# Top-32 attention and a tanh-shrink layer: GpSimd computes a step's threshold ahead of the preceding step's row sums, VectorE its reciprocal ahead of the selection rounds

## The chip, the cores and the metric

The kernel runs on one core of one Trainium2 chip. A core has TensorE (PE, matrix products into PSUM), VectorE (DVE), ScalarE (ACT), GpSimd (POOL) and SyncE (SP, which issues most DMAs). Each engine works through its own list of instructions in order, and semaphores make one engine wait for another. The metric is the time of one execution in device microseconds (us), as the median of several runs.

## The reference, cut to what matters

Batch 8, 8 heads, 576 rows, head width 64; the layer behind it has 4608 rows of 512, an inner width of 2048, and everything is float32.

```
scores = scale * np.matmul(q, k.transpose(0, 1, 3, 2))            # 576 x 576 per head
kth = np.partition(scores, -top_k, axis=-1)[..., -top_k:-top_k + 1]   # top_k = 32
scores = np.where(scores >= kth, scores, -1000000000.0)
scores = scores - np.max(scores, axis=-1, keepdims=True)
attn = np.exp(scores); attn = attn / (np.sum(attn, axis=-1, keepdims=True) + 1e-09)
attn_out = np.matmul(attn, v)
x = attn_out.transpose(0, 2, 1, 3).reshape(B * S, H * D)
h = x @ w_in
out = (h - np.tanh(h)) @ w_out
```

So every row of scores needs its 32nd largest value, and all that is below it is dropped before the softmax.

## The kernel before, in words

The work is cut into 144 steps. A step takes 128 rows of queries for a pair of heads, so its scores are a tile of 128 partitions by 2 x 576. The loop over n at L991 writes the instructions out by hand, in an order in which several steps are under way at once; what is recorded there is the order in which every engine works. In one turn n:

- `mask(n - 1)` (L386): GpSimd forms the threshold tb (L396, one instruction for each head of the pair) and the negative row maximum nb (L405) from the maxima m. ScalarE turns score and tb into a penalty with a Relu (L409), GpSimd subtracts it from the scores (L412), and then compares the selection's bounds with tb (bad, L416).
- `search(n)` (L340): VectorE forms pairwise maxima and minima of the scores (L359 to L367), takes the eight largest of six pieces (L371), and then runs four rounds of MAX8 (L378) and MATCH_REPLACE8 (L381), which give the 32 largest in m. After round i it calls `between(i)`. After round 0 that is `invert(n - 2)`, VectorE's reciprocal of the row sums (L451), and `divide(n - 2)`, ScalarE's multiplication by it (L458); after the last round it is `turn_z(n - 2)`, VectorE's block transpose of the result (L490).
- pieces of the feed-forward part, dealt by `deal` in portions of 0.4, 0.2, 0.2 and 0.2 of what is due in a step. They are matmuls (L606, and L719 for the second product, which is done in seven products of quarters), ScalarE's tanh and copy (L618, L619), GpSimd's subtraction (L620), its sums of quarters (L693) and its joins (L740).
- `scores(n + 1)` (L317): TensorE writes the scores of the next step into a single PSUM tile (L329), which VectorE frees at L367; ScalarE copies it to SBUF (L337).
- `expo(n - 1)` (L428): ScalarE's exponentials with row sums (L432), and GpSimd's addition of 1e-9 to the sums, which goes into rd (L442).
- every second step `values` (TensorE, L555) with weights that went out to DRAM and back through SP's queue in another order.

The steps of the first batch (`pe` is true, up to about 240 us) go another way after the exponentials: TensorE transposes them (L527), the reciprocal is L448, it is spread by GpSimd (L471), and GpSimd multiplies the result (L573). In that stretch the weights are also converted (L182 to L205).

The order on an engine matters here in this way: before the change GpSimd meets, between the subtraction of one step and the threshold of the next, first the bad comparison, then feed-forward work of the first portion, then rd of the step before, then feed-forward work of the later portions, and then tb:

```
            if here(-1):
                mask(n - 1, exact)          # tb, nb, Relu, subtraction of step n - 1
            if here(0):
                search(n, exact, between)   # m of step n
            ...
            if here(1):
                scores(n + 1)
            ...
            if here(-1):
                expo(n - 1)                 # exponentials and rd of step n - 1
```

## Time and profile before

| what | us |
|---|---|
| median of 3 runs | 1554.77 (1550.6 to 1556.14) |
| the profiled execution | 1556.96 |
| its span, first to last instruction | 1555.2 |
| mask on ScalarE, L409, x288 | 0.774 each (median) |
| threshold on GpSimd, L396, x288 | 0.300 each (median) |
| nb on GpSimd, L405, x144 | 0.248 each (median) |
| subtraction on GpSimd, L412, x288 | 1.413 each (median) |
| rd on GpSimd, L442, x144 | 0.227 each (median) |
| reciprocal on VectorE, L451, x126 | 0.151 each (median) |
| division on ScalarE, L458, x252 | 0.760 each (median) |
| transpose on VectorE, L490, x126 | 1.359 each (median) |

The times of single instructions come from the profiled execution, which is a little longer than the median. Busy times are shares of the span, and in a row of waits the first number is the sum of idle time in us before the instructions of a line, the second how often, the third the longest. In rows of the timeline the first number is the start, the second the duration of all that is merged in the row, and the bracket the idle time before it with what ended it. A step takes about 9.2 us in the middle of the kernel.

### The profile page before, as it was taken

How to read it: one execution, taken by the hardware profiler on the slowest of the kernel's cores; microseconds unless marked ns; L12 is line 12 of the kernel's file. 1: busy time of each engine (PE TensorE's matmuls, PEld its weight loads, DVE VectorE, ACT ScalarE, POOL GpSimd, SP SyncE). 2: the span in 40 equal slices, each digit the busy share in tenths (PEclk: the TensorE clock that was granted, in tenths of full speed). 3: DMA queues.
4: the chain of work that ended last, by engine and by line, in shares of the span. 5: the costliest groups of instructions: out<-in, count | busy, mean ns of one | idle time of the engine just before them, and what ended most of it. 6: DMA issues, size and time to landing. Idle time of an engine off the chain costs nothing.

```text
span 1555.2 us, 26814 instructions
## 1 busy us (share of the span) xinstructions
PE 1404.2 (90%) x7892; PEld 1068.5 (69%) x7892; DVE 1296.3 (83%) x4914; ACT 1015.9 (65%) x1898; POOL 1103.7 (71%) x1573
## 2 busy tenths in 40 slices
PE   4677997899998999989989999999998989999998
PEld 2455655666766767766767777777776767778887
DVE  7998898899999999898988899989999888883000
ACT  4766775776776767776766777777776766674311
POOL 3777689868677686858686868686877686767523
PEclk9778999999999999999999999999999999999999
DMA  9945113677667576575766666667575666643311
GB/s 264 365 172 176 26 34 106 157 192 161 187 158 189 145 167 166 155 198 139 191 156 164 158 173 159 172 153 197 150 180 149 156 153 160 169 142 95 96 44 43
DMA packets 257178, 241.70 MB, mean 155 GB/s; under 512 B 193536, under 2 KB 201728, under 8 KB 249856
## 3 DMA queue, kind: packets, MB, share of 16 engines
q1 hardware_dynamic: 255248, 239.69, 58.0%
q8 instruction: 65, 1.06, 0.3%
q14 instruction: 89, 0.73, 0.2%
q10 hardware_dynamic: 1776, 0.22, 0.1%
HBM read 153.99 MB, written 85.85 MB: 154 GB/s over the span
## 4 chain that ended last, share of the span: by engine, by line
PE 30%; DVE 26%; POOL 16%; ACT 16%; issue 5%; DMA 5%; SPq 0%; DVEq 0%; ACTq 0%; POOLq 0%
PE hps L606 11%; PE hx L719 6%; PE hy L719 6%; DVE m L378 4%; POOL g L620 4%; ACT z L458 4%; DVE top L371 4%; ACT z L409 4%; POOL z L412 4%; POOL g L693 3%; PE av L555 3%; PE scps L329 3%; DVE zx L490 3%; ACT z L432 3%; DVE rest L381 3%
## 5 line engine op out<-in xcount | busy, mean ns | idle before, releaser
L606 PE MATMUL hps<-xT,w_in 128*128 128x256 f32 (+1 forms) x2176 | 479.1, 377 | 11.5 <-ACT g L619 10.3
L606 PEld LDWEIGHTS hps<-xT,w_in 128*128 128x128 f32 x2176 | 396.9, 195 | 92.0 <-issue 23.5
L412 POOL TENSOR_TENSOR z<-sc,z 128x576 f32<-128x576 f32 x288 | 404.6, 1427 | 74.2 <-ACT z L409 74.2
L409 ACT ACTIVATE z<-sc,tb 128x576 f32<-128x576 f32 x288 | 207.6, 768 | 246.7 <-POOL tb L396 232.6
L620 POOL TENSOR_TENSOR g<-g,th 128x512 f32<-128x512 f32 x144 | 183.2, 1273 | 100.4 <-ACT g L619 99.4
L490 DVE STREAM_TRANSPOSE zx<-z 128x1152 f32<-128x1152 f32 x126 | 172.0, 1365 | 88.6 <-ACT z L458 86.5
L432 ACT ACTIVATE z<-z,nb 128x576 f32<-128x576 f32 x288 | 221.8, 776 | 2.3 <-POOL z L412 2.3
L458 ACT ACTIVATE z<-z,rd 128x576 f32<-128x576 f32 x252 | 180.4, 763 | 55.2 <-DVE rd L451 53.7
L329 PE MATMUL scps<-kT,qT 64*128 64x288 f32 (+1 forms) x1120 | 161.6, 439 | 42.4 <-DVE top L367 35.6
L371 DVE MAX8 top<-ab 128x8 f32<-128x144 f32 x864 | 193.9, 292 | 0.0
L337 ACT COPY sc<-scps 128x1152 f32<-128x1152 f32 x144 | 160.7, 1116 | 21.2 <-PE scps L329 20.8
L378 DVE MAX8 m<-rest 128x8 f32<-128x168 f32 x576 | 160.2, 318 | 0.0
L329 PEld LDWEIGHTS scps<-kT,qT 64*128 64x128 f32 (+1 forms) x1120 | 88.5, 180 | 96.9 <-issue 29.4
L442 POOL TENSOR_SCALAR rd<-den 128x2 f32<-128x2 f32 x144 | 32.7, 227 | 171.4 <-ACT z L432 165.0
L378 DVE MAX8 m<-top 128x8 f32<-128x144 f32 (+1 forms) x576 | 150.5, 301 | 0.0
L719 PE MATMUL hx<-w_out,g 128*128 128x256 f32 x544 | 134.9, 396 | 9.9 <-POOL g L620 7.0
L719 PEld LDWEIGHTS hx<-w_out,g 128*128 128x128 f32 x544 | 104.0, 196 | 38.2 <-POOL g L620 11.7
L719 PE MATMUL hy<-more,g 128*128 128x256 f32 x544 | 130.0, 391 | 0.1
L719 PEld LDWEIGHTS hy<-more,g 128*128 128x128 f32 x544 | 105.1, 196 | 21.7 <-issue 4.6
L618 ACT ACTIVATE th<-hps 128x512 f32<-128x512 f32 x144 | 84.3, 586 | 53.8 <-PE hps L606 51.4
L365 DVE TENSOR_TENSOR ab<-scps,sc 128x576 f32<-128x576 f32 x144 | 107.4, 746 | 0.0
L555 PE MATMUL av<-spare,vb 128*64 128x256 f32 (+1 forms) x1056 | 97.4, 327 | 0.0
(116 smaller groups left out, 2356.1 us busy)
## 6 DMA issues: line engine op xcount, KB each, us to landing
there<-zx SPq DMA_DIRECT2D x56, 1152.0 KB, 4.7
spare<-there SPq DMA_DIRECT2D x224, 288.0 KB, 5.5
more<-kept_T SPq DMA_DIRECT2D x34, 512.0 KB, 3.9
kin<-in_k_dram SPq DMA_DIRECT2D x116, 72.0 KB, 3.6
out_dram<-ot SPq DMA_DIRECT2D x32, 256.0 KB, 3.0
there<-zx SPq DMA_DIRECT2D x14, 576.0 KB, 7.1
spare<-there SPq DMA_DIRECT2D x56, 144.0 KB, 3.2
vb<-in_v_dram SPq DMA_DIRECT2D x48, 128.0 KB, 4.9
```

The lines of the kernel that those rows point to most:

```text
L329: nc.tensor.matmul(ps[rows, t, s, 0:S2], qT[g.b, g.hp + i, g.part][half(t), qs], kT[g.b, g.hp + i][half(t), ks], start=True, stop=True,)
L337: nc.scalar.copy(sc[:], ps[:, :, :, 0:S2])
L371: nc.vector.max(top[:, t, o : o + 8], low[:, t, i, :])
L378: nc.vector.max(m[:, t, m8], seen[i][t])
L409: nc.scalar.activation(zv[:, t, :], scf[:, t, :], AF.Relu, bias=tb[:, t : t + 1], scale=-BIG)
L412: nc.gpsimd.tensor_tensor(zv[:, t, :], scf[:, t, :], zv[:, t, :], ALU.subtract)
L432: nc.scalar.activation(x["zv"][:, t, :], x["zv"][:, t, :], AF.Exp, bias=x["nb"][:, t : t + 1], scale=scale, accum_out=den[:, t : t + 1],)
L458: nc.scalar.activation(x, x, AF.Copy, scale=rds[n][:, g.i, t : t + 1])
L490: nc.vector.transpose(tiles(zx, g.nq)[:, :, :, g.i, :].rearrange("p c k j -> p k c j"), z[:].rearrange("p (k c j) -> p k c j", c=NG, j=G),)
L606: nc.tensor.matmul(cur[u][:, s : s + w], w_in[j][:, c, fo : fo + P], u.xT[:, c, 0:w], start=(c == 0), stop=(c == CD - 1),)
L620: nc.gpsimd.tensor_tensor(g, g, th[:], ALU.subtract)
L719: nc.tensor.matmul(acc, lhs[:, m, :], rhs, start=(fresh and k == 0 and m == 0), stop=(k == 1 and m == 3), skip_group_check=True)
```

## The change

`mask` is split in two. The instructions for tb and nb become a function `threshold`, which is called for step n after `scores(n + 1)` and before `expo(n - 1)`, so GpSimd meets tb and nb of step n directly before rd of step n - 1. What is left of `mask` stays where it was, one turn later. For steps that are not of the first batch, the reciprocal of step n - 2 is recorded in `search(n)` before the first round and no longer behind it; the division stays behind the first round in the recorded order, and its order on ScalarE is as before.

```diff
--- before.py
+++ after.py
@@ -372,6 +372,7 @@
             seen = [[top[:, t, 0:S4] for t in range(2)], [top[:, t] for t in range(2)]]
             seen += [[rest[:, t] for t in range(2)]] * (rounds - 2)
             left = [seen[0], *seen[2:]]
+        between(-1)
         for i in range(rounds):
             m8 = slice(8 * i, 8 * i + 8)
             for t in range(2):
@@ -383,11 +384,10 @@
 
     bad = consts.tile([P, 2, B * NHP * J + 2 * B, NL], U8, name="bad")
 
-    def mask(n, exact):
+    def threshold(n, exact):
 
         x = st[n]
-        sc, m = x["sc"], x.pop("m")
-        scf = sc[:].rearrange("p t s k -> p t (s k)")
+        m = x.pop("m")
         tb = mpool.tile([P, 2], FP32, tag="tb", name="tb")
         if exact:
             nc.gpsimd.tensor_scalar(tb[:], m[:, :, TOP - 1], BIG, None, ALU.mult)
@@ -403,6 +403,12 @@
                 )
         nb = mpool.tile([P, 2], FP32, tag="nb", name="nb")
         nc.gpsimd.tensor_scalar(nb[:], m[:, :, 0], -scale, None, ALU.mult)
+        x.update(tb=tb, nb=nb)
+
+    def mask(n, exact):
+
+        x = st[n]
+        tb, scf = x["tb"], x["sc"][:].rearrange("p t s k -> p t (s k)")
         z = zpool.tile([P, 2 * S], FP32, tag="z", name="z")
         zv = z[:].rearrange("p (t k) -> p t k", t=2)
         for t in range(2):
@@ -421,7 +427,7 @@
                     ALU.mult,
                     ALU.is_gt,
                 )
-        x.update(z=z, zv=zv, nb=nb)
+        x.update(z=z, zv=zv)
 
     rds = {}
 
@@ -940,11 +946,14 @@
         def between(i):
             for fn in at_round.pop((n, i), []):
                 fn()
-            if i == 0 and here(-2):
+            if not here(-2):
+                return
+            pe = steps[n - 2].pe
+            if i == (0 if pe else -1):
                 invert(n - 2)
-                if not steps[n - 2].pe:
-                    divide(n - 2)
-            if i == LATE and here(-2) and not steps[n - 2].pe:
+            if i == 0 and not pe:
+                divide(n - 2)
+            if i == LATE and not pe:
                 turn_z(n - 2)
 
 
@@ -1006,8 +1015,8 @@
             if here(0):
                 search(n, exact, between)
             elif here(-2):
-                between(0)
-                between(LATE)
+                for i in (-1, 0, LATE):
+                    between(i)
             if pe:
                 spread(n - 2)
             deal(0.0 if pe else 0.4)
@@ -1020,6 +1029,8 @@
                 scores(n + 1)
             if pe:
                 next(w)
+            if here(0):
+                threshold(n, exact)
             if here(-1):
                 expo(n - 1)
             deal(0.8 if pe else 0.2)
```

## The prediction

> **What bounds the kernel now.** I read the page's busy shares first, then the busy time by stage, then the waits of all engines, then one step in the timeline. On the page no engine is full over the whole span:

> ```profile
> PE 1404.2 (90%) x7892; PEld 1068.5 (69%) x7892; DVE 1296.3 (83%) x4914; ACT 1015.9 (65%) x1898; POOL 1103.7 (71%) x1573
> ```

> The average hides the stages, so I cut the span into stretches (busy us of each engine, then clock and DMA):

> ```profile
> 0.00:240.00 240.00, 177.48 (x1078) 123.60 (x1079) 212.75 (x769) 160.69 (x303) 166.97 (x246) 0.88 0.54 169
> 240.00:600.00 360.00, 317.17 (x1760) 234.96 (x1759) 337.74 (x1292) 251.99 (x465) 271.37 (x398) 0.96 0.65 166
> 600.00:800.00 200.00, 188.85 (x1070) 142.56 (x1069) 187.81 (x730) 143.34 (x266) 149.24 (x216) 0.99 0.65 165
> 800.00:1380.00 580.00, 554.14 (x3185) 426.60 (x3184) 525.22 (x2011) 401.91 (x750) 431.71 (x626) 0.98 0.64 164
> 1380.00:1556.00 176.00, 166.61 (x806) 140.82 (x805) 32.81 (x115) 57.99 (x117) 84.44 (x90) 0.98 0.26 75
> ```

> The reader is to see three regimes. In 240 to 600 VectorE is the fuller engine (22.3 us idle) and TensorE has 42.8 us idle. In 600 to 800 both have some 12 us. In 800 to 1380 TensorE is the fuller (25.9 us idle) and VectorE has 54.8. After 1380 TensorE works off what is left of the feed-forward part and nothing in the attention part can shorten that. ScalarE and GpSimd have a quarter or more idle everywhere, so their idle time counts only where it is passed on. The list of waits says how (waited in all, times, longest):

> ```profile
> ACT z L409 <- POOL tb L396: 232.6, 116, 6.2
> POOL rd L442 <- ACT z L432: 165.0, 97, 5.3
> DVE zx L490 <- ACT z L458: 86.5, 50, 8.9
> ACT z L458 <- DVE rd L451: 53.7, 39, 2.4
> PE scps L329 <- DVE top L367: 35.8, 18, 4.9
> DVE scps L359 <- ACT sc L337: 33.1, 35, 3.8
> ```

> ScalarE's mask waits 232.6 us for the thresholds tb. ScalarE's next instruction is the division of the step before it (L458), and VectorE's transpose (L490) waits 86.5 us for that division. A late VectorE then makes TensorE wait in the scores (35.8 us), since the PSUM tile of the scores comes free at L367. One step of the timeline shows why tb is late:

> ```profile
> 723.83 0.56 DVE L378 MAX8 m<-rest 128x8 f32<-128x168 f32 x2
> ...
> 729.28 0.23 POOL L442 TENSOR_SCALAR rd<-den 128x2 f32<-128x2 f32 x1
> 729.41 0.50 DVE L378 MAX8 m<-top 128x8 f32<-128x144 f32 x2
> 729.59 1.26 POOL L693 TENSOR_TENSOR g<-et,g 128x512 f32<-128x512 f32 x1
> 730.38 0.15 DVE L451 RECIPROCAL rd<-rd 128x2 f32<-128x2 f32 x1
> 730.81 1.27 POOL L693 TENSOR_TENSOR g<-g 128x512 f32<-128x512 f32 x1
> 732.04 0.72 POOL L740 TENSOR_TENSOR ot<-ot,oy 128x256 f32<-128x256 f32 x1
> 732.76 0.58 POOL L396 TENSOR_SCALAR tb<-m 128x1 f32<-128x1 f32 x2
> 733.09 1.44 ACT L409 ACTIVATE z<-sc,tb 128x576 f32<-128x576 f32 x2 [6.01 <-POOL tb L396]
> 734.44 1.42 ACT L458 ACTIVATE z<-z,rd 128x576 f32<-128x576 f32 x2
> 735.90 1.38 DVE L490 STREAM_TRANSPOSE zx<-z 128x1152 f32<-128x1152 f32 x1 [2.75 <-ACT z L458]
> ```

> The maxima that tb needs were complete at 724.39; tb ran at 732.76, behind rd (which had waited for ScalarE's exponentials), two sums and a join of the feed-forward part. ScalarE stood still for 6.01 us and handed 2.75 of them to VectorE.

> **The change part by part.** The orders of instructions as built, before against after, agree on TensorE, ScalarE and the DMA queue of SP; only GpSimd and VectorE differ, and no instruction is added, removed or resized, and no DMA moves. All that changes is who waits.

> *The threshold goes ahead of rd (GpSimd).* Two tb and one nb, 0.58 + 0.24 = 0.82 us by the rows, now stand directly before L442 in place of directly before the subtractions L412; they are moved past rd and past every subtraction (L620), sum (L693) and join (L740) that is dealt later in the step. Example above: tb could start at 729.2, the mask at about 729.5, its end at 731.0, the division 731.0 to 732.4, and VectorE's rounds end at 733.15. The wait of 2.75 is gone. I take the same for the other waits of L490 on L458, by stage (DVE's waits in the stage, then what TensorE can follow):
> - 240 to 600: 20.5 us in 14 waits. VectorE is the bound here and TensorE has room (28.3 us of its 42.8 are waits for the scores' buffers, 23.5 of them for L367). I count 17, since the last fraction of a shortened wait goes to whatever is next.
> - 600 to 800: 9.1 us, against 11.1 us idle of TensorE (3.5 of it for L367, 3.9 for the sums of GpSimd, which start earlier when the mask does). I count 6.
> - 800 to 1380: 35.3 us, and some of the 15.3 in which L359 waits for the scores' copy. But TensorE has only 25.9 us idle: 8.5 for L367 and 17.2 for GpSimd and ScalarE (L693 9.3, L620 5.7, L619 2.2). Taking the 8.5 and a tenth of the rest: 10.
> - 1380 on: 21.6 us of L490's waits, counted 0; TensorE runs here 166.61 of 176 us.
> - 0 to 240: the tb wait is 10.5 us of ScalarE's time, in seven waits, and no wait of VectorE stems from it; the joins of this stage (L573) go behind a wait for the selection. Bounds -5 and +6, counted 0.

> *The same place makes a new wait.* GpSimd now stands before tb until the selection of the same step has ended; behind it are rd, the subtractions of the feed-forward part and the sums that TensorE's products read. From the trace I took, for the 122 steps from 240 to 1400, when GpSimd was done with what precedes rd, and when the last MAX8 ended: in 96 steps the maxima were there first (so no wait), in 26 GpSimd came first, by 33.2 us in all, half of it in two steps. Cover: in those 26 rd itself waited for the exponentials, and 0.82 us of threshold fits into that wait. Where it does not, the 0.82 us falls on rd and on the sums behind it: in the example the product that waits 0.90 for a sum would wait 1.7. TensorE's waits for L693 are 12 in number, 17.4 us; 12 x 0.82 = 10 at worst, and below nothing when the mask and with it the subtractions come about 1.2 us earlier, as they do wherever tb had been waiting. Bounds -10 and +8; I take a loss of 2.

> *The reciprocal goes ahead of the rounds (VectorE).* 126 of them, 0.15 us each, move past two MAX8 and two MATCH_REPLACE8: from 730.38 to about 729.4, so 1.0 us. ScalarE's division waits 53.7 us for it in 39 places, and with tb early it would wait for it more often; 1.0 us sooner covers part. The cost: VectorE can now stand before all four rounds if rd is late. In those 122 steps rd was ready 1.9 us (median) before the first MAX8; with 0.82 us of threshold in front of it 11 steps would be short, by 8.5 us in all. Bounds 0 and 8.5; the earlier mask makes the exponentials and rd earlier too, so I take a loss of 2.

> The sum: 17 + 6 + 10 - 2 - 2 = 29 us. The profiled execution took 1556.96 us (span 1555.2), 2.2 above the median, and becomes 1528; against the median, 1554.77 - 29 = 1526.

> [...] Row: PE is busy 554.14 of 580 us in 800 to 1380 by its matmuls, 426.60 by its weight loads. [...] By the row TensorE has 25.9 us. I follow the row: in the solid run at 1441 it takes 26.17 us for 120 of these matmuls, 0.22 each, and the 32 at 704.24 took 7.17, the same 0.22, so inside its busy stretches it goes at the pace of the tail, where nothing delays it.

> **The rivals.**
> *TensorE is the bound everywhere that matters.* The FFN work is dealt by steps, and a VectorE that runs ahead meets it at the scores. For: 95% after 800. Against: 23.5 us waited for L367 before 600. Then only about half of the first two stages comes, 0 to 15 us, about 8: 1547.
> *All waits fall.* If sums and copies come earlier too, TensorE's idle time goes down to the gaps of its queue: 42 of 80 us before 1380 plus a few in the start, gain 50: 1505. For: its waits on GpSimd and ScalarE are ends of the same loop. Against: freed waits are seldom freed whole.
> *The new wait decides (slower).* GpSimd's stand before tb reaches TensorE through the sums L693 and subtractions L620. Price: the 33.2 us of the 26 steps and their 26 x 0.82 = 21, together 54, against the 29: 25 slower, 1580. It decides from 29 / 122 = 0.24 us of added wait for GpSimd's results in a mean step. For: TensorE already waits for L693 and L620 at 18 places, so there is no stock of sums. Against: in 96 of 122 steps the maxima were there first.
> *It does not do what it says.* It could not act if tb waited for the selection itself; the waits of L409 on MAX8 are 7.8 us against 232.6 on tb, so this has almost no chance.

> **How the numbers follow.** About 0.5% (7.8 us) is what a measurement of this kernel can tell from no change. The forecast (gain 15 to 45): 0.62. All waits fall: 0.08. TensorE bound: 0.18, half of it within 0.5%. The new wait decides: 0.12, of which 0.02 stays within 0.5%. Faster 0.62 + 0.08 + 0.09 = 0.79; same 0.09 + 0.02 = 0.11; slower 0.10. The range goes from 1506 (nearly all waits) to 1550 (TensorE bound); the slower case and the lower part of the TensorE case stay outside.

> **What would show it.** Right: the wait of the mask on tb falls from 232.6 to under 60 us, that of L490 on L458 from 86.5 to under 35, ScalarE's division waits longer for the reciprocal (over 53.7), VectorE's idle time in 240 to 600 falls below 10 us, and in the late stage TensorE is above 97%. The reciprocal's wait for rd, 3.2 us now, stays below 10. Wrong: a new GpSimd wait for MAX8 of over 50 us together with longer waits of the products for L693 or L620 (then the slower case), or VectorE's wait moved from L490 to L359 with TensorE at 95% as before (then TensorE was the bound).

## The result and the profile after

The changed kernel takes 1499.69 us (median of 4 runs, 1498.83 to 1501.18) against 1555.45 before: a ratio of 0.9648, 95% interval 0.9625 to 0.9671. The gain is 55.8 us, about double the 29 that were forecast, and the time lies below the range (1506 to 1550). The direction and the mechanism were right; one term of the sum was far too small. In what follows, the changed kernel's lines have moved by 1 to 6, so L409 of before is L415 after, L490 is L496, L442 is L448, L693 is L699.

The page's busy shares of the changed kernel:

```profile
PE 1382.9 (92%) x7892; PEld 1060.6 (71%) x7892; DVE 1293.6 (86%) x4914; ACT 1023.5 (68%) x1898; POOL 1102.4 (74%) x1573
```

The number of matmuls is the same to the last one, yet TensorE's busy time fell by 21.3 us (1404.2 before). That is the line that the prediction had no room for. The stretches, with the same columns as before:

```profile
0.00:240.00 240.00, 179.27 (x1095) 124.28 (x1097) 218.19 (x780) 165.22 (x311) 171.24 (x251) 0.89 0.54 169
240.00:600.00 360.00, 327.43 (x1850) 245.59 (x1846) 351.16 (x1359) 265.42 (x485) 280.42 (x412) 0.97 0.69 175
600.00:800.00 200.00, 193.24 (x1104) 148.21 (x1104) 192.95 (x749) 148.03 (x273) 159.17 (x231) 0.99 0.67 171
800.00:1380.00 580.00, 572.66 (x3321) 448.45 (x3314) 527.28 (x2025) 418.48 (x775) 446.62 (x644) 1.00 0.64 167
```

VectorE is now full in 240 to 600 (351.16 of 360) and TensorE in 800 to 1380 (572.66 of 580, at a granted clock of 1.00 where it had been 0.98). The waits that the change was about (us in all, times, longest):

```profile
ACT z L464 <- DVE rd L457: 92.2, 65, 2.8
POOL rd L448 <- ACT z L438: 74.3, 66, 4.9
...
DVE scps L359 <- ACT sc L337: 35.1, 28, 4.6
POOL tb L396 <- DVE m L379: 34.5, 25, 3.3
...
PE scps L329 <- DVE top L367: 30.0, 17, 4.7
...
ACT z L415 <- POOL tb L396: 25.8, 17, 3.9
...
DVE zx L496 <- ACT z L464: 18.8, 6, 8.9
...
DVE rd L457 <- POOL rd L448: 13.8, 10, 4.0
```

The mask's wait for tb went from 232.6 to 25.8 us, VectorE's transpose now waits 18.8 instead of 86.5, and ScalarE's new place to stand, that is to wait with nothing to run, is the reciprocal (92.2 after 53.7), of which little reaches VectorE. GpSimd has the new wait for the last maxima, 34.5 us. The step of the timeline that the prediction showed, at the same point of the work:

```profile
698.95 0.57 DVE L379 MAX8 m<-rest 128x8 f32<-128x168 f32 x2
...
702.62 1.28 POOL L699 TENSOR_TENSOR g<-g 128x512 f32<-128x512 f32 x1
...
703.89 0.58 POOL L396 TENSOR_SCALAR tb<-m 128x1 f32<-128x1 f32 x2
704.23 1.44 ACT L415 ACTIVATE z<-sc,tb 128x576 f32<-128x576 f32 x2 [1.19 <-POOL tb L396]
...
704.76 0.23 POOL L448 TENSOR_SCALAR rd<-den 128x2 f32<-128x2 f32 x1
705.02 0.17 DVE L457 RECIPROCAL rd<-rd 128x2 f32<-128x2 f32 x1 [0.40 <-POOL rd L448]
705.07 1.27 POOL L699 TENSOR_TENSOR g<-et,g 128x512 f32<-128x512 f32 x1
...
705.58 1.43 ACT L464 ACTIVATE z<-z,rd 128x576 f32<-128x576 f32 x2
...
706.40 1.99 PE L725 MATMUL hx<-et,g 128*128 128x256 f32 x8 [1.68 <-POOL g L699]
...
708.70 1.36 DVE L496 STREAM_TRANSPOSE zx<-z 128x1152 f32<-128x1152 f32 x1
```

tb runs ahead of the two later sums and the join. ScalarE waits 1.19 us for it instead of 6.01, and the transpose follows the rounds without a wait (2.75 before). The price is there too: the reciprocal stands 0.40 us for rd, and the product at 706.40 waits 1.68 us for its sum (0.90 before).

For a table by stage I took VectorE's pair-wise operation L365, which stands near the head of every step, as a mark, so that the same work is compared:

| steps | before, us | after, us | gain | forecast |
|---|---|---|---|---|
| start to 20 | 232.3 | 228.6 | 3.7 | 0 |
| 20 to 60 | 373.7 | 357.7 | 16.0 | 17 |
| 60 to 80 | 187.4 | 179.9 | 7.4 | 6 |
| 80 to 143 | 619.4 | 588.4 | 31.0 | 10 |
| 143 to the end | 142.4 | 142.3 | 0.1 | 0 |
| added waits | | | in the above | -4 |

The sum is 58.2 us between the two profiled executions. (The run below that is unlike before only from step 80 on reached the marks up to step 80 within 1.0 us of before, so 3.7 in the start is more than that difference.) Two terms hit; that of steps 80 to 143 was a third of what came.

### The profile page after: what moved, and what is told of

The parts are those of the page before. It is cut to its first block, busy times and chain, and to the rows that moved or that the text cites. A ratio compares the mean times of both kernels' runs of the same rounds, so it can differ in the third digit from the quotient of the medians.

```text
span 1497.0 us, 26829 instructions
## 1 busy us (share of the span) xinstructions
PE 1382.9 (92%) x7892; PEld 1060.6 (71%) x7892; DVE 1293.6 (86%) x4914; ACT 1023.5 (68%) x1898; POOL 1102.4 (74%) x1573
## 4 chain that ended last, share of the span: by engine, by line
PE 55%; DVE 22%; POOL 5%; DMA 3%; ACT 2%; issue 2%; SPq 1%; DVEq 0%; ACTq 0%; POOLq 0%
PE hps L612 23%; PE hx L725 10%; PE hy L725 7%; PE av L561 7%; PE scps L329 6%; DVE m L379 4%; DVE zx L496 3%; DVE top L371 3%; DVE rest L382 3%; DVE ab L365 2%; POOL z L418 2%; POOL g L699 1%; DVE ab L360 1%; DMA kin<-in_k_dram 1%; DVE top L382 1%
## 5 line engine op out<-in xcount | busy, mean ns | idle before, releaser
L612 PE MATMUL hps<-xT,w_in 128*128 128x256 f32 (+1 forms) x2176 | 472.8, 374 | 5.8 <-ACT g L625 5.5
L626 POOL TENSOR_TENSOR g<-g,th 128x512 f32<-128x512 f32 x144 | 183.6, 1275 | 116.9 <-ACT g L625 115.8
L464 ACT ACTIVATE z<-z,rd 128x576 f32<-128x576 f32 x252 | 181.1, 767 | 92.4 <-DVE rd L457 92.2
L415 ACT ACTIVATE z<-sc,tb 128x576 f32<-128x576 f32 x288 | 208.2, 775 | 29.8 <-POOL tb L396 25.8
L337 ACT COPY sc<-scps 128x1152 f32<-128x1152 f32 x144 | 160.7, 1116 | 51.7 <-PE scps L329 51.4
L496 DVE STREAM_TRANSPOSE zx<-z 128x1152 f32<-128x1152 f32 x126 | 171.7, 1363 | 21.9 <-ACT z L464 18.8
L329 PE MATMUL scps<-kT,qT 64*128 64x288 f32 (+1 forms) x1120 | 158.7, 431 | 32.8 <-DVE top L367 30.0
L329 PEld LDWEIGHTS scps<-kT,qT 64*128 64x128 f32 (+1 forms) x1120 | 87.4, 178 | 86.7 <-ACT z L415 31.8
L725 PE MATMUL hx<-w_out,g 128*128 128x256 f32 x544 | 131.1, 391 | 0.6 <-POOL g L626 0.4
L725 PE MATMUL hy<-more,g 128*128 128x256 f32 x544 | 125.9, 382 | 0.0
L725 PEld LDWEIGHTS hy<-more,g 128*128 128x128 f32 x544 | 102.1, 190 | 19.3 <-issue 5.8
L396 POOL TENSOR_SCALAR tb<-m 128x1 f32<-128x1 f32 x288 | 83.8, 299 | 35.1 <-DVE m L379 34.5
L365 DVE TENSOR_TENSOR ab<-scps,sc 128x576 f32<-128x576 f32 x144 | 107.7, 748 | 0.0
```

Of the source, the lines that this page charges most:

```text
L329: nc.tensor.matmul(ps[rows, t, s, 0:S2], qT[g.b, g.hp + i, g.part][half(t), qs], kT[g.b, g.hp + i][half(t), ks], start=True, stop=True,)
L415: nc.scalar.activation(zv[:, t, :], scf[:, t, :], AF.Relu, bias=tb[:, t : t + 1], scale=-BIG)
L464: nc.scalar.activation(x, x, AF.Copy, scale=rds[n][:, g.i, t : t + 1])
L496: nc.vector.transpose(tiles(zx, g.nq)[:, :, :, g.i, :].rearrange("p c k j -> p k c j"), z[:].rearrange("p (k c j) -> p k c j", c=NG, j=G),)
L612: nc.tensor.matmul(cur[u][:, s : s + w], w_in[j][:, c, fo : fo + P], u.xT[:, c, 0:w], start=(c == 0), stop=(c == CD - 1),)
L626: nc.gpsimd.tensor_tensor(g, g, th[:], ALU.subtract)
```

## The experiments

My theory after the result: the ceiling of the late stage was set wrongly. Idle time of TensorE is not all that a wait costs; after a stand (a stretch in which TensorE waits with nothing to run) the granted clock can fall to 0.50 (for 3.41 us from 1193.41 of before, behind a stand of 2.67), and that lies in the busy time. The rival is that the ceiling was right, and the surplus came from somewhere else, such as the reciprocal. A second question was which of the two moves, and which of the things that tb was moved past, made the gain.

**Only the threshold moved.**

```diff
-            if i == (0 if pe else -1):
+            if i == 0:
                 invert(n - 2)
```

> Only the threshold moves; the reciprocal stays behind the first round. If the threshold is the whole of it (the wait of the mask on tb is what was passed on to VectorE), the time is 1500 to 1510. If the reciprocal carries a third of the gain because ScalarE's division then waits for it instead of for tb, the time is about 1520, and VectorE's transpose still waits over 30 us for the division.

Measured: 1505.19 us (before, measured beside it: 1557.19), ratio 0.967, interval 0.9643 to 0.9697. The transpose waits 18.8 us for the division, as in the whole change. So the threshold carries nearly all of the gain. ScalarE waits 138.5 us for the reciprocal here, 46.3 more than in the change, and none of the addition reaches the transpose. The interval overlaps that of the whole change, so what the reciprocal adds on top of it is not settled.

**Only the reciprocal moved.** tb and nb stay in front of the subtractions:

```diff
+                threshold(n - 1, exact)
                 mask(n - 1, exact)
...
-            if here(0):
-                threshold(n, exact)
```

> Only the reciprocal moves; tb and nb stay directly before the subtractions. If the threshold is the whole of the gain: 1550 to 1560, the wait of the mask on tb stays near 230 us. If the division's wait for the reciprocal (53.7 us before) had been passed on: 1540 or less. If VectorE now stands for rd: above 1560.

Measured: 1547.43 us, ratio 0.9942, interval 0.9923 to 0.9962, so 9.8 us below 1557.19, between two of the expectations. VectorE's waits in this run:

```profile
DVE zx L496 <- ACT z L464: 75.2, 46, 8.9
...
DVE rd L457 <- POOL rd L448: 4.0, 4, 1.7
```

The earlier reciprocal lets the division run earlier where tb did not hold it, which takes 11.3 us off the transpose's waits, and it makes VectorE stand only 4.0 us for rd (3.2 before). I had counted this move as a loss of 2. Alone it is a small gain; 52.0 for the threshold alone and 9.8 for this add to 6.0 more than the 55.8 of both, but the intervals are as wide as that, so whether the two share a part is not settled.

**The threshold behind rd, ahead of the later feed-forward work.**

```diff
-            if here(0):
-                threshold(n, exact)
             if here(-1):
                 expo(n - 1)
+            if here(0):
+                threshold(n, exact)
```

> The threshold goes behind rd of the preceding step, but stays ahead of the later portions of feed-forward work; the reciprocal is moved as in the change. If the feed-forward work in front of tb was the delay: within 8 us of the change, 1492 to 1508. If rd with its wait for the exponentials (165 us before) was the delay: at least half of the gain is lost, 1527 or more.

Measured: 1501.93 us, ratio 0.9652, interval 0.9624 to 0.968: the same as the change. That tb goes ahead of the row sums, the words of the change, has no measurable part in the gain. What counts is that it goes ahead of the feed-forward subtractions, sums and joins that are dealt behind them.

**The threshold directly behind the search.**

```diff
                 search(n, exact, between)
+                threshold(n, exact)
```

> The threshold goes directly behind the search, ahead of all feed-forward portions of the step, so GpSimd stands for the maxima with subtractions and sums behind it. If GpSimd's stand before tb is what hurts (the slower rival of the prediction): slower than the change by 20 us or more, GpSimd's wait for MAX8 over 100 us and TensorE's waits for the sums over 20 us. If earlier is simply better: 1490 or less. If tb is already early enough: within 8 us of 1500.

The call in its later place is taken out. Measured: 1513.24 us, ratio 0.9724, interval 0.9708 to 0.9741, so some 13 us slower than the change. GpSimd's waits in this run:

```profile
POOL tb L396 <- DVE m L379: 79.9, 47, 3.3
```

This is the slower rival of the prediction: GpSimd stands for the maxima with feed-forward work behind it. It exists, and it sets how far ahead tb should go. It fell short of the numbers that I had set for it: a wait of 100 us, 20 us of TensorE's waits for the sums L699 (12.9, against 7.3 in the change) and a loss of 20. By the marks 7 of the 13 us were lost by step 24, in the start; what took them there was not looked into.

**The change from step 80 on.** For earlier steps both instructions stay where they were:

```diff
-            if here(0):
+            if here(0) and n >= 80:
                 threshold(n, exact)
...
+                if n - 1 < 80:
+                    threshold(n - 1, exact)
                 mask(n - 1, exact)
...
-            if i == (0 if pe else -1):
+            if i == (0 if pe or n < 80 else -1):
```

> Both moves for the steps from 80 on only, which begin at about 793 us of 1555. By the prediction's sum the idle time of TensorE is the ceiling there and 10 us come back: 1545. If TensorE's busy time itself falls, because the clock that it is granted halves after each stand of some 2 us and more (the records show five such dips after 800 us before the change and none after it), the whole difference between steps 80 and 143 comes back, 31 us: 1524.

Measured: 1527.79 us, ratio 0.9815, interval 0.9788 to 0.9842: 29.4 us below 1557.19. Steps 80 to 143 of before, and then of this run (us, then busy us of PE, PEld, DVE, ACT, POOL, clock, DMA):

```profile
793.40:1412.80 619.40, 591.79 (x3379) 456.14 (x3378) 552.65 (x2119) 427.51 (x798) 456.60 (x657) 0.98 0.62 160
```

```profile
792.40:1382.70 590.30, 579.81 (x3379) 450.41 (x3378) 550.88 (x2119) 431.48 (x798) 457.13 (x660) 1.00 0.65 168
```

The stage gives its 29.1 us with the rest as before: the ceiling of the prediction was wrong, and nothing from the earlier stages was needed. The two rows divide it: 3379 matmuls in both, TensorE's idle time 27.6 to 10.5, so 17.1, and its busy time 591.79 to 579.81, so 12.0 more. In the whole change the same steps read

```profile
766.30:1354.70 588.40, 579.89 (x3381) 451.25 (x3380) 550.66 (x2119) 430.09 (x795) 455.96 (x659) 1.00 0.65 169
```

that is 19.1 of idle time and 11.9 of busy time, together 31.0.

What the busy part is can be seen before the change in the timeline of TensorE near 1190 us, and in the stretch that holds the second product:

```profile
1185.81 1.99 PE L719 MATMUL hy<-w_out,g 128*128 128x256 f32 x8
1187.64 1.89 PE L719 MATMUL hx<-more,g 128*128 128x256 f32 x8
1192.20 2.61 PE L719 MATMUL hx<-et,g 128*128 128x256 f32 x8 [2.67 <-POOL g L693]
1194.61 3.00 PE L719 MATMUL hy<-more,g 128*128 128x256 f32 x8
```

```profile
1194.60:1197.60 3.00, 3.00 (x11) 2.18 (x10) 3.00 (x20) 1.92 (x4) 2.59 (x5) 0.62 1.00 191
```

The sixteen matmuls of the first two rows take 3.72 us, from 1185.81 to 1189.53. After a stand of 2.67 us for a sum, the sixteen of the last two rows take 5.41, from 1192.20 to 1197.61, with a mean granted clock of 0.62 in the stretch from 1194.60: 1.7 us more. A stand of 2.67 thus cost 4.4. The trace's clock records have five such dips to a granted clock of 0.50 between steps 80 and 143 before the change, 20.5 us long together (half of that is 10.2, most of the 11.9 to 12.0; the rest is not accounted for), and none after it. Over the whole span the half-speed time fell from 116.0 to 77.0 us.

**A forced stand.** To add stands and leave the rest as it is, the changed kernel gets a tiny matmul (8 columns of weights), a small DMA over its operand, and the matmul again, at the head of each of the 17 second products:

```diff
+    def stand(acc):
+        def touch():
+            nc.tensor.matmul(acc[0:8, 0:64], stand_in, w_out[0][:, 0, 0:64], start=True, stop=True, skip_group_check=True)
+        touch()
+        for _ in range(1):
+            nc.sync.dma_start(stand_in, v[0, 0, 0:P, 0:8])
+            touch()
...
             cur[u] = [next_h("hx"), None]
+            stand(cur[u][0])
```

> The changed kernel, with one forced stand of TensorE at the head of the second product of each of the 17 full units: a small matmul, a small DMA that overwrites its operand, and the small matmul again, which must wait for the DMA (some 2 to 3 us each, by the few us that DMAs take to land in the trace). If idle time is all that a stand costs, TensorE's busy time stays at 1383 us (within 3) and the time grows by no more than the added waits. If each stand also halves the granted clock for 3.4 us, busy time grows by about 1.7 us for each, to 1405 to 1412, and the low-clock time in the records after 230 us grows from 24 us to about 80.

Measured: 1589.47 us, 90 more than the change, and more than the 71.5 us of added waits. Its busy shares and the wait that was added:

```profile
PE 1416.7 (89%) x7960; PEld 1079.2 (68%) x7960; DVE 1294.3 (81%) x4914; ACT 1023.9 (64%) x1898; POOL 1103.8 (69%) x1574
```

```profile
PE hx L713 <- DMA stand_in<-in_v_dram: 71.5, 17, 7.0
```

TensorE's busy time did not stay: it grew by 33.8 us, of which its own 34 pairs of tiny matmuls are 9.5 (0.28 us a pair at full clock). The other 24 us are 1.4 for each stand, a little less than the 1.7 expected, and the half-speed time rose by 85.6 us, to 162.6, in part of which TensorE stood. The stands were longer than expected (71.5 / 17 = 4.2 us), because SP's queue often came late to the DMA: this took 2.3 us (median) from issue to landing, but at 1032.28, for one, it was issued 3.5 us after TensorE had begun to stand. The rival "idle time only" is refuted: by it, busy time would have grown by no more than the 9.5 us of added instructions.

**Two stands, one behind the other** (`range(2)` above).

> As the one before, with two such round trips one behind the other, so a stand of about double the length. Idle alone: the further growth over the single stand equals the further waits, busy time as before. Clock: as some dips in the records are 3.4 us long and some 6.8, a longer stand either keeps 1.7 us of busy time for each (dip of one length) or doubles it to 3.4 (busy time 1430 or more).

Measured: 1627.61 us. The waits are 100.4 us, busy time 1429.7, so 46.8 over the change, of which 14.3 are the 51 pairs at full clock: 1.9 us for each place. The waits are 1.40 times those of the run before, and what the clock costs is 1.34 times as much (32.5 us after 24.3), so it grew about as the waits did. The 1.9 lies between the two forms that I had set (1.7 and 3.4), nearer to the first, and doesn't decide between them.

**More feed-forward work early.** VectorE is full in 240 to 600 while TensorE still has 32.6 us idle, so the changed kernel deals more there:

```diff
-            return max(low, high)
+            return max(low, high) * (1.15 if 20 <= n < 70 else 1.0)
```

> The changed kernel with 1.15 times the feed-forward work dealt in each of the steps 20 to 69, where TensorE still has 32 us idle between 240 and 600 us and VectorE is full, so that less is left for the end, where TensorE alone works. If TensorE's idle time there can be filled without delaying VectorE: 10 to 25 us less than the change, 1475 to 1490. If the added work makes the scores late: 1500 or more.

Measured: 1496.88 us, ratio 0.9618, interval 0.9602 to 0.9634. It is the lowest median of all, but the interval overlaps that of the change, and the two were not measured beside each other. Its own marks are 4.6 us late at step 40 and level at step 96. Not the 10 us that I had hoped for; whether it is a gain at all stays open.

## Why the prediction was wrong, by its own steps

- *tb waits in GpSimd's queue behind feed-forward work, and the wait ends up at VectorE's transpose.* Right, and shown from both sides: tb alone gives 1505.19, and with rd ahead of it but the feed-forward work behind it nothing is lost (1501.93).
- *Steps up to 80: 17 and 6.* Measured 16.0 and 7.4. Where VectorE was the bound, its waits were the right measure.
- *Steps 80 on: "TensorE has only 25.9 us idle ... Taking the 8.5 and a tenth of the rest: 10".* This is the step that failed; it came to 31. Two errors are in it. First, of the 17.2 us that TensorE waited there for GpSimd and ScalarE I let a tenth go. In the same steps, 80 to 143 by the marks, these waits fell from 18.9 to 6.3 (L699 3.6, L626 0.4, L625 2.3), and those for L367 from 8.5 to 2.3, which is nearly all of the 19.1 by which TensorE's idle time fell. I read it so: a mask that comes earlier lets the subtraction, the comparison and then the sums come earlier, on the very queue that TensorE waited for; no run tests this by itself. Second, I took busy time for work. 11.9 us of it went away with the same number of matmuls, most of it (10.2) the half clock of the five dips behind such waits. The evidence lay in the rows that I quoted: a granted clock of 0.98 in a stage in which TensorE was nearly full.
- *"I follow the row."* The row, with its 25.9 us of idle time, gave 1526, and 1499.69 came. I argued from the pace in two solid runs, where the granted clock was 1.00 (704.24 to 711.41, and 1441 to 1467), and not from the rows behind a stand, where it was not (0.62 from 1194.60). TensorE was the fuller engine, as the row had it: it ran up to 98.7% busy in matmuls from 800 to 1380, with VectorE at 91%. But its idle time did not bound the gain.
- *The new wait, a loss of 2.* GpSimd waits 34.5 us for the maxima, about the 33.2 that were taken from the trace of before, but TensorE's waits for the sums L693 fell in total from 17.4 to 7.3. The single sum in the step shown was late by what the prediction said (1.68 against 1.7).
- *The reciprocal, a loss of 2.* Alone it gains 9.8; what it adds to the threshold is not settled. It stands 13.8 us for rd, above the 10 that I set as a limit, but 6.8 of that is in the last two steps, where TensorE alone decides.
- *The start, 0.* It gained 3.7, inside the bounds.
- *The rivals.* "All waits fall" (1505) was the nearest and had 0.08, but only its number was near: it took the whole gain of 50 from TensorE's idle time, which fell by 36.9 over the span (151.0 to 114.1); the other 21.3 came out of busy time, for which no case had a place. "TensorE is the bound" erred in the same point. The slower one is real, but only for an earlier place (1513.24).

## What to carry to other kernels

An instruction on which another engine waits should stand in its queue directly where its input becomes ready, ahead of bulk work that nobody awaits so soon, but no earlier: with tb directly behind the search GpSimd stood 79.9 us for the maxima, with its later work behind it, and the kernel was 13 us slower than the change. When a gain seems bounded by an engine's idle time, read its granted clock in the same stage: in steps 80 to 143 TensorE was busy 591.79 of 619.40 us at 0.98, and of the 31.0 us that came back 11.9 lay in that busy time. Look at what the freed engine feeds next as well: with the mask's wait for tb (232.6 to 25.8 us) TensorE's waits for the sums, on the same queue, fell from 17.4 to 7.3.

## What the runs showed of the hardware

Before the change, a stand of TensorE of 2.67 us (from 1189.53) was followed by a granted clock of 0.50 from 1193.41 to 1196.82: the sixteen matmuls behind it took 5.41 us in place of 3.72. The length of a stand alone did not decide. Before the change one of 1.88 us (to 1376.63) was followed by a dip from 1377.76, and in the changed kernel stands of 2.74, 2.93 and 2.29 us (to 280.96, 315.11 and 1331.98) were not, so "each stand of some 2 us and more", as I had put it, is too wide. In the run with one forced stand, stands of 1.69 and 1.79 us (from 877.62 and 1552.17) were followed by a dip in the clock, while stands of 2.61 and 2.92 us (from 717.62 and 635.73) were not.

```profile
1189.99:1193.41 3.42, 1.21 (x6) 1.08 (x7) 3.39 (x8) 2.22 (x6) 3.25 (x6) 1.00 0.83 299
1193.41:1196.82 3.41, 3.41 (x10) 2.69 (x9) 3.41 (x21) 1.14 (x3) 3.10 (x6) 0.50 1.04 262
1196.82:1200.23 3.41, 3.41 (x28) 2.04 (x28) 2.94 (x10) 2.27 (x5) 3.32 (x4) 1.00 0.21 32
```

```profile
876.20:879.61 3.41, 1.72 (x23) 0.79 (x21) 3.41 (x12) 2.99 (x7) 2.79 (x7) 1.00 0.02 1
879.61:883.03 3.42, 3.42 (x8) 2.74 (x9) 3.38 (x13) 0.51 (x2) 1.52 (x2) 0.50 0.89 345
```

```profile
633.84:637.25 3.41, 1.89 (x10) 1.24 (x8) 3.38 (x11) 2.41 (x6) 1.73 (x6) 1.00 1.03 205
637.25:640.67 3.42, 2.02 (x10) 1.72 (x11) 3.42 (x21) 2.05 (x4) 3.42 (x3) 1.00 0.04 3
```

The stand of 1.69 us lies in one stride, which leaves 1.72 us of work, and the next stride is at half clock. The stand of 2.92 us falls into two strides, 1.52 and 1.40, and no dip follows (1.00 in the stride behind it as well). Counted from 240 us on over before and after: of 15 full-clock strides in which TensorE stood for 2.0 us or more (10 and 5), all 15 were followed by half clock; of 702 with less than 1.65 us (351 and 351), none; of the 11 between (7 and 4), 4 (3 and 1). The count was made on traces that were there already; no run was built to test it, and what sets the clock is not shown.
